# Packing the global queries of two heads into one block, w_in by halves of rows, and a new sequence of all work, in a kernel of sparse attention and a softplus layer

## The chip, the cores and the metric

The kernel runs on one core of a Trainium2 chip. TensorE (PE) multiplies, and loads its weights beside that (PEld). VectorE (DVE), ScalarE (ACT) and GpSimd (POOL) do the rest; SyncE (SP) and GpSimd issue the DMA transfers. The metric is the device time of one execution in microseconds. The time before is 339.93 us, the median of three runs (339.21, 339.93 and 340.64).

## The reference

```python
def _attn_ref(q, k, v, global_idx):           # B=8, H=8, S=576, D=64; 8 global positions
    scores = scale * np.matmul(q, k.transpose(0, 1, 3, 2))       # scale = 1/sqrt(64)
    mask = np.abs(pos[:, None] - pos[None, :]) <= 32             # a band
    mask = mask | is_global[:, None] | is_global[None, :]        # and 8 global rows and columns
    scores = np.where(mask, scores, -1000000000.0)
    scores = scores - np.max(scores, axis=-1, keepdims=True)
    attn = np.exp(scores)
    attn = attn / (np.sum(attn, axis=-1, keepdims=True) + 1e-09)
    return np.matmul(attn, v)
...
x = attn_out.transpose(0, 2, 1, 3).reshape(B * S, H * D)         # 4608 x 512
h = x @ w_in                                                     # 512 x 2048
g = np.maximum(h, 0.0) + np.log1p(np.exp(-np.abs(h)))            # softplus
return g @ w_out                                                 # 2048 x 512
```

So most queries see a band of 32 keys on either side and the 8 global keys; the 8 global queries of each head see all 576 keys.

## The kernel before

**Tiles.** A sequence of 576 tokens is cut into 18 blocks of 32. The 128 partitions hold four quarters of 32; the eight heads lie as four heads c in one half of a tile and the heads c+4 in the other. The 4608 tokens are worked through in nine phases of 512. A phase has four groups n of 128 tokens, and for each group: scores `s` (L1049) of 32 queries against their band and the global keys, mask added by VectorE (`st`, L1053), maximum `m` (L1066), subtraction (GpSimd, L1072), exponential (ScalarE, L1089), sum `sm` (L1096), reciprocal `rs` (L1098), normalization to `pn` (L1104, on GpSimd or VectorE), transpose to `pt` (VectorE, L1113). When a phase's four groups are there, PE makes the values `xo` (L1216), which are copied to `xT` (L700); then `h` (L1251, with w_in), softplus `g` (ScalarE, L1257), `o` (L1262, with w_out), a copy to `osb` and the store (L1274). The first two phases are cut into smaller pieces so that they can begin earlier, and the first four groups go another way, with the mask put into the scores by PE (L1033, L1043).

**Global queries.** Once a batch, `sg` (L941) multiplies the global queries `qg` with all keys `kx`. A quarter of rows holds the 8 queries of one head, in a block of 32 of which 8 are used; the heads of the second half (g = 1) stand in quarters rotated by one (`a ^ g`), and go to score tiles of their own. Maximum `gm` (L951), exponential `pg` (L958), transpose to `pgt` (L963), a step that writes a 1 at each global position into eight columns more (`own`, L965), then `ov` (L974), which gives the result of the global queries and, by those columns, the values at the global keys. Both become `vg`, which `xo` uses.

**Loads.** Queries, keys and values come in float32 by SP and are cast to bfloat16 (`qb`, `kb`, `vb`; L697, L695, L700, on whichever engine the order names). Batches 0 and 1 come in parts of tokens (L494, L498) and are transposed on PE (`tr`, L829; the global ones picked by `pick`, L835); the others come whole (L444, L449), are transposed by VectorE (L798, L802) and picked on PE (L858, L871). w_in (four quarters of 512 of its 2048 columns, L1313) and w_out (four quarters of rows, L1317) are issued by GpSimd. Some copies exist only to make an engine wait: on GpSimd one for a part of v of batch 0 (L1330), with the w_in issues behind it, and one for the second part of k of batch 1 (L1394), with the w_out issues behind it. On SP a tiny transfer, `trail` (L737), waits for the second quarter of w_in ahead of batch 1, and another for the first quarter of w_out ahead of batch 1's values. Matmuls `warm` (L709) fill PE's idle time at the start.

**The order.** No loop sets the order. Each piece of work is added to a list as a job, with the jobs that it needs and the buffers that it opens and uses. The tuple `ORDER` then holds numbers (5 times the job's number plus its engine), and `run` places the jobs in that sequence, each behind the last one of its engine. A model of durations in `run` decides only which PSUM bank a job gets, how many `warm` matmuls fill a gap, and in which sequence instructions are written; no engine waits for a modelled time.

## Time and profile before

| | us |
|---|---|
| runs | 339.21, 339.93, 340.64 |
| profiled execution, its span | 339.5 |
| PE busy | 319.3 (94%) |
| DVE busy | 250.8 (74%) |
| ACT busy | 222.9 (66%) |
| POOL busy | 170.9 (50%) |

A line of the page's groups reads: line of the kernel, engine, operation, output and inputs by name, partitions by elements and type, count; busy time in all, mean ns of one; idle time of the engine just before them and what ended most of it. In the timeline a row is a run of like instructions: start, length, engine, line, operation, tiles, count, and in brackets the idle time before it and what released it. "issue" there means that the profile shows nothing that the engine waited for. A busy PE is modelled, since matmuls are pipelined. Queue q0 is GpSimd's transfers, q1 is SP's, q8 the fetching of instructions.

### The profile page before, as it was taken

To read this page: it belongs to the slowest core of one execution; us is meant where nothing else is said; L and a number is where in the kernel's file an instruction comes from. 1 tells how busy PE (TensorE), PEld (TensorE's weight loads), DVE (VectorE), ACT (ScalarE), POOL (GpSimd) and SP (SyncE) were. 2 spreads that over 40 slices of the span, in tenths; PEclk is the share of its full clock that TensorE was granted. 3 is DMA by queue.
4 is the path that set the end of the run, shared out by engine and by line. 5 is a ranking of instruction groups with operands and counts; after the bars stand their busy time and mean duration, and the time that the engine had idled before them with its cause. 6 is when DMAs were issued, how large, how long until landed. Compare 5 with 4: busy or idle time off the path is not lost.

```text
span 339.5 us, 12213 instructions
## 1 busy us (share of the span) xinstructions
PE 319.3 (94%) x5336; PEld 169.4 (50%) x5336; DVE 250.8 (74%) x416; ACT 222.9 (66%) x457; POOL 170.9 (50%) x156
## 2 busy tenths in 40 slices
PE   7685967999999998999999999999999999999996
PEld 3434755466555443454455446444544554445443
DVE  7795657996798799989988979898896993441000
ACT  5695744998695757477857683768476738925442
POOL 7384705985387865715966037663514575300000
PEclk9969999999999999999999999999999999999999
DMA  7999999898946999886999995053000022001002
GB/s 183 221 179 232 207 205 171 133 192 136 152 75 105 224 182 200 143 152 130 201 174 235 168 152 133 33 119 87 4 3 31 33 93 83 16 31 66 31 15 109
DMA packets 168733, 42.74 MB, mean 126 GB/s; under 512 B 153192, under 2 KB 165736, under 8 KB 168680
## 3 DMA queue, kind: packets, MB, share of 16 engines
q1 hardware_dynamic: 160664, 28.33, 48.0%
q0 software_dynamic: 6144, 10.49, 13.0%
q10 hardware_dynamic: 1872, 3.15, 2.5%
q8 instruction: 41, 0.67, 0.8%
q14 instruction: 12, 0.10, 0.1%
HBM read 36.71 MB, written 9.44 MB: 136 GB/s over the span
## 4 chain that ended last, share of the span: by engine, by line
PE 78%; SPq 9%; DMA 7%; issue 3%; DVE 1%; ACT 1%; ACTq 0%; POOLq 0%
PE o L1262 35%; PE h L1251 32%; SPq L444 5%; PE xo L1216 4%; DMA stage<-in_v_dram 3%; PE s L1049 3%; DMA win<-in_moe_w_in_dram 2%; DMA stage<-in_k_dram 2%; PE ov L974 2%; SPq L449 1%; SPq L498 1%; DVE qb L695 1%; PE pick L858 1%; PE tr L829 1%; SPq L494 1%
## 5 line engine op out<-in xcount | busy, mean ns | idle before, releaser
L1251 PE MATMUL h<-xT,win 128*128 128x512 bf16 (+3 forms) x768 | 135.8, 326 | 4.0 <-issue 2.3
L1262 PE MATMUL o<-wout,g 128*128 128x512 bf16 (+1 forms) x592 | 136.6, 374 | 0.0
L1257 ACT ACTIVATE g<-h 128x512 bf16<-128x512 f32 (+3 forms) x192 | 85.6, 501 | 44.7 <-PE h L1251 42.7
L1251 PEld LDWEIGHTS <-win 128*128 128x128 bf16 x768 | 66.7, 98 | 63.5 <-issue 5.2
L1262 PEld LDWEIGHTS <-g 128*128 128x128 bf16 x592 | 55.7, 98 | 61.4 <-issue 1.1
L1104 POOL TENSOR_TENSOR pn<-st,rs 128x1024 bf16<-128x1024 f32 (+1 forms) x33 | 57.2, 1745 | 50.4 <-DVE rs L1098 31.8
L1072 POOL TENSOR_TENSOR st<-st,m 128x1024 f32<-128x1024 f32 x24 | 46.6, 1952 | 52.5 <-DVE m L1066 50.1
L1053 DVE TENSOR_TENSOR st<-s,mask 128x512 f32<-128x512 f32 x64 | 41.2, 678 | 12.5 <-PE s L1049 12.4
L1096 DVE TENSOR_REDUCE sm<-st 128x8 f32<-128x1024 f32 x32 | 38.2, 1195 | 7.7 <-ACT st L1089 7.7
L1066 DVE TENSOR_REDUCE m<-st 128x8 f32<-128x1024 f32 x32 | 37.9, 1199 | 0.1
L1089 ACT ACTIVATE st<-st 128x1024 f32<-128x1024 f32 x32 | 33.1, 1059 | 5.8 <-DVE st L1072 4.8
L1113 DVE STREAM_TRANSPOSE pt<-pn 128x512 int32<-128x512 int32 x36 | 24.9, 694 | 6.2 <-POOL pn L1104 6.1
L700 ACT COPY osb<-o 128x512 f32<-128x512 f32 (+1 forms) x29 | 16.7, 576 | 16.8 <-PE o L1262 15.1
L700 ACT CAST xT<-xo 128x512 bf16<-128x512 f32 (+3 forms) x27 | 11.5, 477 | 18.7 <-PE xo L1216 18.6
L700 POOL CAST vb<-stage 128x1152 bf16<-128x1152 f32 x14 | 16.9, 1215 | 9.1 <-PE xo L1216 5.4
L1049 PE MATMUL s<-kx,qx 64*32 64x128 bf16 x1152 | 15.2, 224 | 4.4 <-issue 2.6
L700 DVE CAST xT<-xo 128x512 bf16<-128x512 f32 (+3 forms) x21 | 11.3, 567 | 10.2 <-PE xo L1216 10.1
L1049 PEld LDWEIGHTS <-qx 64*32 64x32 bf16 x1152 | 10.7, 92 | 12.5 <-issue 9.9
L697 POOL TENSOR_SCALAR qb<-stage 128x1152 bf16<-128x1152 f32 (+2 forms) x12 | 12.8, 1074 | 4.7 <-DMA stage<-in_q_dram 2.4
L958 ACT ACTIVATE pg<-sg,gnb 128x320 bf16<-128x320 f32 (+1 forms) x32 | 15.0, 588 | 0.0
L1274 POOL DMA_DIRECT2D out_dram<-osb x24 | 14.7, 615 | 0.0
L951 DVE TENSOR_REDUCE gm<-sg 128x1 f32<-128x320 f32 (+1 forms) x32 | 12.3, 446 | 3.2 <-PE sg L941 3.2
(125 smaller groups left out, 311.3 us busy)
## 6 DMA issues: line engine op xcount, KB each, us to landing
stage<-in_v_dram SPq DMA_DIRECT2D x64, 144.0 KB, 4.0
stage<-in_k_dram SPq DMA_DIRECT2D x48, 144.0 KB, 4.1
stage<-in_q_dram SPq DMA_DIRECT2D x48, 144.0 KB, 3.9
out_dram<-osb POOLq DMA_DIRECT2D x24, 256.0 KB, 3.6
out_dram<-osb ACTq DMA_DIRECT2D x11, 256.0 KB, 2.0
stage<-in_k_dram SPq DMA_DIRECT2D x4, 512.0 KB, 8.2
stage<-in_q_dram SPq DMA_DIRECT2D x4, 512.0 KB, 5.5
win<-in_moe_w_in_dram POOLq DMA_DIRECT2D x4, 512.0 KB, 7.0
```

What stands on the lines that cost most here:

```text
L700: {"ACT": nc.scalar.copy, "DVE": V.tensor_copy, "POOL": nc.gpsimd.tensor_copy}[e](out, in_)
L1049: nc.tensor.matmul(out=PS["s", n, g][quad(a ^ g), x, :], lhsT=qx[b % 2][rows(g), a, j * BL:(j + 1) * BL], rhs=kx[b % 2][rows(g), a, e0 * B ...
L1053: V.tensor_tensor(out=PS["st", n][:, h, :, :], in0=PS["s", n, h][:, :, :], in1=mask[:, h, j0:j0 + PB, :, :].rearrange("p j s i -> p j (s i ...
L1066: V.reduce_max(out=m[:], in_=flat(PS["st", n], h0, h1), axis=AX)
L1072: on(e).tensor_tensor(out=t, in0=t, in1=over(PS["m", n, y][:], SL * BL), op=OP.subtract)
L1089: nc.scalar.activation(out=t, in_=t, func=AF.Exp)
L1096: V.reduce_sum(out=sm[:], in_=flat(PS["st", n], h0, h1), axis=AX)
L1104: on(e).tensor_tensor(out=PS["pn", n][:, :, :, h0:h1].rearrange("p x s h -> p h x s"), in0=PS["st", n][:, h0:h1], in1=PS["rs", n, y][:].re ...
L1113: V.transpose(out=bass.AP(base.tensor, base.offset, ap=[list(base.ap[0]), [2 * STEP, PB // 2], [STEP + BL // 2, 2], [1, SL * BL]]), in_=PS ...
L1251: nc.tensor.matmul(out=h[:, :], lhsT=w_in_t[c // 4][:, kd, c % 4 * P:(c % 4 + 1) * P], rhs=PS["xT", m][:, kd, lo:hi], start=(kd == 0), sto ...
L1257: nc.scalar.activation(out=PS["g", m, c][:, lo:hi], in_=PS[key][:, lo_of(c, hi - lo)], func=AF.Softplus)
L1262: nc.tensor.matmul(out=PS["o", m, ns, a][:, :], lhsT=PS["g", m, kf][:, ns * P:(ns + 1) * P], rhs=w_out_t[kf // 4][:, kf % 4, a:z], start=( ...
```

## The change

1. *Packing.* The heads c and c+4 stand in the same quarter c. Their global queries are the columns 0 to 7 and 8 to 15 of one block of 32, each multiplied by 1 on its own half of the partitions and by 0 on the other (a small constant, `side`, or two copies on ScalarE). One `sg` matmul of 128 rows then gives the scores of both heads: 8 matmuls a batch for 16, 2 score tiles for 4, 2 maxima for 4, 2 exponentials for 4. `pg` and `pgt` have half the columns; the weights of `ov` are read from it with a step of two.
2. *w_in.* Since a quarter c now gives heads c and c+4 to one tile of `xo`, the rows of w_in are placed to match, by eight transfers of 64 partitions where there were four of 128.
3. *The order.* ORDER is new throughout. The model that goes with it has new constants, for DMA and for fetching instructions. `warm` matmuls go from 32 to 38.

```diff
         def gev(e):
-            copy(e, qg[i][:, :, 0:NG], PS[qkey][:, QP:QP + HG * NG].rearrange("p (a g) -> p a g", g=NG))
+            x = PS[qkey][:, QP:QP + HG * NG].rearrange("p (a g) -> p a g", g=NG)
+            if e == "DVE":
+                V.tensor_tensor(out=qg[i][:, :, 0:KG].rearrange("p a (h g) -> p a h g", g=NG),
+                                in0=x.unsqueeze(2).to_broadcast([P, HG, 2, NG]),
+                                in1=side[:].unsqueeze(1).unsqueeze(3).to_broadcast([P, HG, 2, NG]), op=OP.mult)
+                return
+            for g in range(2):
+                copy(e, qg[i][rows(g), :, g * NG:(g + 1) * NG], x[rows(g)])
...
             for x, (a0, an) in enumerate(SPANS):
                 for a in range(HG):
-                    for g in range(2):
-                        rhs = kx[i][rows(g), a, (2 + 3 * a0) * BL:(2 + 3 * (a0 + an)) * BL] \
-                            .rearrange("p (c x) -> p c x", c=an)[:, :, 0:D]
-                        nc.tensor.matmul(out=PS["sg", b, g, x][quad(a ^ g), 0:an * D], lhsT=qg[i][rows(g), a, :], rhs=rhs,
-                                         start=True, stop=True)
+                    rhs = kx[i][:, a, (2 + 3 * a0) * BL:(2 + 3 * (a0 + an)) * BL].rearrange("p (c x) -> p c x", c=an)[:, :, 0:D]
+                    nc.tensor.matmul(out=PS["sg", b, x][quad(a), 0:an * D], lhsT=qg[i][:, a, :], rhs=rhs, start=True, stop=True)
...
-    pg = const([P, NJ, BL, 2], BF16, "pg")
+    pg = const([P, NO, BL, 2], BF16, "pg")
...
     def weights_in(x):
-        nc.gpsimd.dma_start(out=w_in_t[x][:, :, :],
-                            in_=moe_w_in.rearrange("(a p) f -> p a f", p=P)[:, :, x * WC:(x + 1) * WC])
+        for g in range(2):
+            nc.gpsimd.dma_start(out=w_in_t[x][rows(g), :, :],
+                                in_=moe_w_in.rearrange("(g a d) f -> g d a f", g=2, d=D)[g, :, :, x * WC:(x + 1) * WC])
...
-        42, 47, 116, 92, 9, 121, 126, 111, 132, 52, 107, 137, 102, 97, 143, 83, 148, 158, 87, 152, 178, 14, 221, 19,
...
```

What the new order does is read from the instructions of the two programs. GpSimd, from the w_in issues to the first subtraction, before (the tile win_124 is w_in's first quarter, wout_128 w_out's; stage_61 holds k, stage_60 q, stage_62 v):

```order
25 L1313 DMA win_125<-in_moe_w_in_dram 128x4x512
26 L700 CAST vb_66<-stage_62 128x18x64 x2
27 L1313 DMA win_126<-in_moe_w_in_dram 128x4x512
28 L1104 TENSOR_TENSOR pn<-st,rs 128x512 x3
29 L1313 DMA win_127<-in_moe_w_in_dram 128x4x512
30 L1104 TENSOR_TENSOR pn<-st,rs 128x512 x3
31 L513 MEMSET kx_71 128x40x16
...
35 L1394 COPY seen<-stage_61 128x1
36 L700 CAST kb<-stage_61 128x2x4x64
37 L1317 DMA wout_128<-in_moe_w_out_dram 128x4x512
```

and of the change:

```order
26 L1245 DMA win_130<-in_moe_w_in_dram 64x4x512 x2
27 L1245 DMA win_131<-in_moe_w_in_dram 64x4x512 x2
28 L652 CAST vb_66<-stage_62 128x18x64
29 L1245 DMA win_132<-in_moe_w_in_dram 64x4x512 x2
30 L1039 TENSOR_TENSOR pn<-st,rs 128x512 x3
31 L1325 COPY seen<-stage_61 128x1
32 L1249 DMA wout_133<-in_moe_w_out_dram 128x4x512
33 L1249 DMA wout_134<-in_moe_w_out_dram 128x4x512
34 L462 MEMSET kx_71 128x40x16
...
39 L1249 DMA wout_135<-in_moe_w_out_dram 128x4x512
40 L652 CAST kb<-stage_61 128x2x4x64 x2
```

All w_in issues now stand ahead of the normalizations of phase 0, the blanking of `kx` behind the copy that waits, and the casts of the second half of batch 1's keys behind three w_out issues instead of ahead of all. The last w_out issue stands behind four casts of q before (row 43), and behind two and the first subtraction now (also row 43).

PE, where batch 1's keys are transposed, before:

```order
882 L1251 MATMUL h<-xT,win_124 128x128
883 L829 LDWEIGHTS kb
884 L829 MATMUL tr<-ident,kb 128x128
...
914 L835 MATMUL pick<-hot,kb 128x8
915 L1251 LDWEIGHTS win_126
```

and of the change:

```order
1044 L1149 MATMUL xo<-pt,vb_66 64x32
1045 L1183 LDWEIGHTS win_131
...
1100 L1183 MATMUL h<-xT,win_132 128x128
1101 L774 LDWEIGHTS kb
1102 L774 MATMUL tr<-ident,kb 128x128
```

The first transposes of batch 1 stood ahead of the second 88 values of phase 0 (rows 929 to 1104), and those of the keys' second half directly behind; now those values (rows 869 to 1044) and 28 h matmuls stand ahead of the transposes, and the second half of the keys follows at row 1150.

SP, at the start, before (k, its small parts, q, its small parts, q, then v):

```order
2 L494 DMA stage_61<-in_k_dram 128x8x128 x2
3 L498 DMA stage_61<-in_k_dram 64x4x64 x2
4 L494 DMA stage_60<-in_q_dram 128x8x128
5 L498 DMA stage_60<-in_q_dram 64x4x64 x2
6 L494 DMA stage_60<-in_q_dram 128x8x128
7 L449 DMA stage_62<-in_v_dram 32x18x64 x8
```

and of the change:

```order
2 L443 DMA stage_60<-in_q_dram 128x8x128
3 L447 DMA stage_60<-in_q_dram 64x4x64 x2
4 L443 DMA stage_61<-in_k_dram 128x8x128
5 L447 DMA stage_61<-in_k_dram 64x4x64 x2
6 L443 DMA stage_61<-in_k_dram 128x8x128
7 L398 DMA stage_62<-in_v_dram 32x18x64 x4
```

q now leads, and half of v comes ahead of the second part of q.

More of the change, by code (lines that the diff above doesn't have):

```diff
@@ L100, in room @@
[L100 to L111 removed]
+            t0 = max(t0, free[want - 1])
+        return t0
@@ new lines, in stall @@
+    def stall(self, t, took, ins):
+        held, n = 0, self.issued
+        asked, need, due, last = self.fetch
+        due = list(due)
+        while n + ins >= min(asked, need):
+            at = min(asked, need)
+            here = t + held + took * max(at - n, 0) / max(ins, 1)
+            if at == asked:
+                ask = max(here, last - self.USABLE)
+                last = ask + self.FETCH + max([0] + [
+                    self.HEAVY if x["queue"] and x["each"] <= 100 else next(wait for each, wait in self.WAIT if x["each"] > each)
+                    for x in self.dma if x["to"] > ask + 200 and x["from"] < ask + 1500])
+                due.append(last)
+                asked += self.BLOCK
+            else:
+                held += max(0, due.pop(0) - here)
+                need += self.BLOCK
+        return held, (asked, need, due, last)
@@ L112, in settle, with advance @@
+    def advance(self, s, until):
+        lines = self.lines
+        while any(s["at"][q] < len(lines[q]) for q in range(2)) and s["now"] < until:
+            due = [1e12, 1e12]
+            for q in range(2):
+                if s["at"][q] < len(lines[q]):
+                    due[q] = max(lines[q][s["at"][q]]["ask"] + self.START[q], s["ok"][q])
+            on = [t <= s["now"] + 1e-9 for t in due]
             if not any(on):
-                now = min(due)
+                if min(due) >= until:
+                    return
+                s["now"] = max(s["now"], min(due))
@@ L121, in settle @@
+            if not any(on):
+                continue
+            rate = [1.0 * x for x in on]
+            if all(on):
+                each = [lines[q][s["at"][q]]["each"] for q in range(2)]
+                rate = [x / sum(each) for x in each]
+            step = until - s["now"]
             for q in range(2):
                 if on[q]:
-                    left[q] -= step * rate[q]
-            now += step
+                    step = min(step, s["left"][q] / rate[q])
+                elif due[q] < 1e11:
+                    step = min(step, max(due[q] - s["now"], 1e-6))
@@ L136, in keep, with transfer @@
+    def transfer(self, j, t):
+        q = int("POOL" in j["cost"])
+        n, each = j["moves"]
+        self.advance(self.base, t - 4000)
+        x = dict(queue=q, ask=t, work=n * each, each=each, job=j if j["lands"] else None, to=1e18)
+        x["from"] = 0
+        self.dma.append(x)
+        self.lines[q].append(x)
+        self.advance({k: list(v) if isinstance(v, list) else v for k, v in self.base.items()}, 1e11)
     def keep(self, t0, t1, order):
@@ L155, in keep @@
         order.append(j)
-    def size(self, j):
-        return j["ins"] or 2
-    def follow(self, places):
-        engines = ("PE", "ACT", "DVE", "POOL", "DMA")
-        self.given = [(x // 5, engines[x % 5]) for x in places]
     def due(self, j):
@@ new lines, in due, with run @@
+        return max(t, self.room(j["opens"])) if j["opens"] else t
+    def run(self, places, free):
+        engines = ("PE", "ACT", "DVE", "POOL", "DMA")
+        order, table, array = [], "exp", 128
+        self.dma, self.lines = [], ([], [])
+        self.base = dict(at=[0, 0], left=[-1, -1], ok=[-1, -1], now=0)
+        self.fetch, self.issued = (self.ASK, self.NEED, [], 0), 0
+        mine, other = (0, 0), (0, 0)
+        for place in places:
+            j, e = self.jobs[place // 5], engines[place % 5]
+            t = max(self.due(j), free[e])
+            step, took = j["cost"][e]
@@ L324 @@
     KG = 2 * NG
+    NO = NJ // 2
     VW = 2 * D + 2
@@ L1402 @@
         make_batch(batches(us)[-1] + 1)
-    o.follow(ORDER)
-    for job in o.run(dict(PE=1200 if WARM else 3000, ACT=2600, DVE=2100, POOL=3400, DMA=2300)):
+    for job in o.run(ORDER, dict(PE=1200, ACT=2600, DVE=2100, POOL=3400, DMA=2300)):
         job["emit"](job["on"])
```

456 lines of the change are left out of this document (175 added, 281 removed), and 133 rows, old and new, of the table ORDER.

## The prediction

> **What bounds the kernel now.** I read the page first: the span, the busy shares and the 40 slices.
>
> ```profile
> span 339.5 us, 12213 instructions
> PE 319.3 (94%) x5336; PEld 169.4 (50%) x5336; DVE 250.8 (74%) x416; ACT 222.9 (66%) x457; POOL 170.9 (50%) x156
> PE   7685967999999998999999999999999999999996
> ```
>
> TensorE is busy for 94% of the span, and the digits below 8 stand only in the first seven slices, which are 8.5 us each. From there on it is the bound. So a change of order can win only what stands idle at the front, and the small gaps behind it. The stretches tell how much that is (us, then busy time and number of instructions of PE, PEld, DVE, ACT, POOL; then PEclk, DMA share, GB/s):
>
> ```profile
> 26.30:44.60 18.30, 14.03 (x348) 11.60 (x340) 11.13 (x28) 12.13 (x48) 9.73 (x18) 1.00 1.15 218
> 44.60:55.02 10.42, 5.62 (x141) 3.93 (x140) 6.02 (x8) 4.23 (x12) 2.92 (x2) 1.00 1.22 197
> 55.02:140.00 84.98, 82.86 (x1648) 46.41 (x1649) 74.78 (x114) 64.38 (x127) 57.70 (x40) 1.00 0.87 155
> 90.00:250.00 160.00, 158.04 (x2860) 79.13 (x2858) 145.42 (x215) 109.31 (x175) 95.43 (x69) 1.00 0.71 136
> ```
>
> Between 26.3 and 55.0 us PE stands idle for 4.3 + 4.8 = 9.1 us, from 55 to 140 us for 2.1 us in all. The last row is a warning: there VectorE is busy for 145.4 of 160 us, the second engine close to its bound.
>
> What the 9.1 us are, by PE's timeline (start, us, engine, line, operation, count, then the idle time before it and what ended it):
>
> ```profile
> 28.52 2.67 PE L1251 MATMUL h<-xT,win 128*128 128x128 bf16 x44 [1.62 <-ACT xT L700]
> 33.41 0.40 PE L829 MATMUL tr<-ident,kb 128*128 128x128 bf16 x4 [2.22 <-DVE kb L700]
> 47.45 0.66 PE L1049 MATMUL s<-kx,qx 64*32 64x128 bf16 x53 [2.63 <-issue]
> 55.02 0.34 PE L1251 MATMUL h<-xT,win 128*128 128x128 bf16 x3 [2.17 <-issue]
> ```
>
> One wait of 2.22 us is for keys of batch 1, which stand ahead of the values of phase 0. Two waits, 2.63 and 2.17 us, end on "issue": PE waited for no other engine. How many instructions PE had issued by then says what they are (stretches from 0):
>
> ```profile
> 0.00:40.80 40.80, 30.71 (x607) 18.64 (x607) 30.66 (x88) 29.40 (x112) 26.97 (x57) 0.92 1.09 207
> 0.00:44.82 44.82, 34.56 (x735) 21.79 (x735) 32.58 (x93) 32.09 (x122) 27.57 (x57) 0.92 1.10 204
> 0.00:52.85 52.85, 39.96 (x863) 25.66 (x863) 37.55 (x101) 35.74 (x132) 28.84 (x58) 0.94 1.12 204
> ```
>
> 607, 735 and 863 of each kind: the steps are 128 + 128 = 256 instructions, exactly. The page's queue of instructions moves 41 packets for 10672 instructions of PE, again about 260 to a packet. So PE runs dry at a block of code that is fetched by DMA. In the windows 44.7 to 47.4 us and 52 to 55 us the queues show why it is late:
>
> ```profile
> q8 instruction: 41, 0.67, 0.8%
> q0 software_dynamic: 547, 0.54, 121.9%
> q8 instruction: 1, 0.02, 2.2%
> q1 hardware_dynamic: 2046, 0.51, 111.7%
> q8 instruction: 1, 0.02, 2.9%
> ```
>
> The first row is the page's, over the span. In each window one packet of code goes through engines that w_out (q0), then v (q1) keep wholly busy. The Trainium skill ("Runtime: NRT & Kernel Launch", section "Instruction fetch mechanics") gives the block as 256 instructions, and the trace agrees; it calls the crossing "mostly hidden", and here two crossings cost 4.8 us.
>
> **The change part by part.** *Packing the global queries.* Four reductions and four exponentials a batch become two and two; the transpose halves from 576 to 288 columns, the maximum behind it too.
>
> ```profile
> L951 DVE TENSOR_REDUCE gm<-sg 128x1 f32<-128x320 f32 (+1 forms) x32 | 12.3, 446 | 3.2 <-PE sg L941 3.2
> L958 ACT ACTIVATE pg<-sg,gnb 128x320 bf16<-128x320 f32 (+1 forms) x32 | 15.0, 588 | 0.0
> L963 DVE STREAM_TRANSPOSE pgt<-pg x9: 446/726/779, 21.3 to 268.1; 128x576 int32<-128x576 int32 x7, 128x320 int32<-128x320 int32 x1, 128x256 int32<-128x256 int32 x1
> L965 DVE TENSOR_REDUCE pgt<-own x9: 285/452/453, 21.8 to 268.9; 128x288 bf16<-128x288 bf16 x7, 128x160 bf16<-128x160 bf16 x1, 128x128 bf16<-128x128 bf16 x1
> L941 PE MATMUL sg<-kx,qg x128: 267/306/436, 15.9 to 262.6; 64*32 64x320 bf16 x64, 64*32 64x256 bf16 x64
> ```
>
> VectorE saves 2 x 0.446 = 0.89 us a batch. The transpose of 288 columns lies next to the one of 256, which is the 446 ns; I take 0.47 for 0.726, so 0.25 us. The maximum goes the same way from 0.452 to about 0.30, 0.15 us. That is 1.3 us a batch, 10 us in all. ScalarE saves 2 x 0.588 = 1.2 us a batch if an activation stays as long (its output is written with a step as before); were it twice as long, nothing. On PE, 16 matmuls on quarter tiles, eight at a time, become 8, four at a time: two rounds either way, so nothing, with bounds from half a round to a round of 0.31 us a batch: -1.2 to +2.5 us. Directly the part is worth zero, since PE does not wait for VectorE there. The order hands the time out again: VectorE gets six more normalizations from GpSimd, so its load stays about equal, and GpSimd's falls by some 10 us.
>
> *w_in by halves of rows.* Eight transfers of 256 KB for four of 512 KB:
>
> ```profile
> L1313 POOL DMA_DIRECT2D win<-in_moe_w_in_dram x4: 751/786/992, 16.2 to 25.0; - x4
> DMA to landing us min/median/max: 5.9/7.0/8.2
> ```
>
> GpSimd pays 4 x 0.786 = 3.1 us more of issuing. The issues now run from about 16.2 to 23, with a cast between, where the last of before was at 25.0, because three normalizations no longer stand ahead of it; the last quarter, 5.9 to 8.2 us later by the row, lands at 29 to 31 us for 31 to 33 before. The first h matmuls, which used two other quarters first and now go through all four, then start at 28.5 to 29.4, at most 0.9 us late; what follows waits for other things (below), so I count 0, with bounds 0 to +0.9. The Trainium skill ("DMA: Bandwidth & Descriptors", section "Rules for kernel authors") speaks against it: two transfers to disjoint halves of the partitions serialize, and one over 128 should be used. By that rule both halves together land when the one did, and the sum keeps only the issuing; no run here shows a split one yet.
>
> *The front.* The values of phase 0 (88 matmuls) now stand ahead of the transposes of batch 1 instead of behind the first of them. Behind 36 h matmuls of 0.061 us (2.67/44) from 29.4 they start at about 32 us, where PE of before stood waiting. So the 2.22 us are filled with work. What comes late next is the second half of batch 1's keys, cast on GpSimd:
>
> ```profile
> 28.76 0.80 POOL L513 MEMSET kx<- 128x640 int32 x3
> 35.01 0.44 POOL L1394 COPY seen<-stage 128x1 f32<-128x1 f32 x1 [5.30 <-DMA stage<-in_k_dram]
> 35.40 0.61 POOL L700 CAST kb<-stage 128x512 bf16<-128x512 f32 x1
> 35.95 2.29 POOL L1317 DMA_DIRECT2D wout<-in_moe_w_out_dram  x3
> 51.58 1.89 POOL L1072 TENSOR_TENSOR st<-st,m 128x1024 f32<-128x1024 f32 x1 [10.18 <-DVE m L1066]
> ```
>
> In the new order GpSimd does: the copy that waits (35.01 + 0.44), two w_out issues (1.53), the memsets that were done at 28.76 before (0.80, and some 0.2 for two small ones), a small cast (about 0.4), a third issue (0.76), the cast (0.61). The sum is 39.8 us. PE asks for it at row 1150 of its order, which it reaches at about 37, so a new wait of up to 3 us stands there. The fetch goes on meanwhile, so that the block at row 1470, for which PE of before waited 2.63 us, is there when PE comes, at 39.8 and 7.6 us of work (rows 1150 to 1470 by the durations of before): about 47.4, the clock of before. But by then the new order has put 2.2 us more work through: 72 and 56 h matmuls of 128 and 256 columns for 64 and 36 (20 x 0.109, half of the 0.217 that 512 columns take, below). At the next block, row 1726, it is 1.3 us ahead (more h, fewer s). That block came 7.5 us behind its forerunner before; with the forerunner at 45 to 47, it is there at 52 to 54.5 for 55.02. So the front wins from 1.3 + 0.5 to 1.3 + 3.1 us, 1.8 to 4.4. I take 2.4, near the low end, since w_out still fills the engines at the same time. Bounds: -1 (w_out's last quarter, issued behind the first subtraction of phase 1, comes late by as much as was won and 1 us more) to +5 (both waits on code gone).
>
> *Behind the front.* Of the 2.1 us idle between 55 and 140 us, GpSimd's lighter load and earlier casts can fill about half: -1.1, bounds 0 to -2.1. The matmuls on small tiles are in fewer groups, 85 for 92 changes of the tile's form after the front. One change is worth what these rows leave:
>
> ```profile
> 56.87 0.38 PE L1262 MATMUL o<-wout,g 128*128 128x512 bf16 x1
> 59.53 2.11 PE L1262 MATMUL o<-wout,g 128*128 128x512 bf16 x9
> 61.57 0.44 PE L941 MATMUL sg<-kx,qg 64*32 64x320 bf16 x16
> 61.94 2.33 PE L1262 MATMUL o<-wout,g 128*128 128x512 bf16 x10
> ```
>
> One o takes 0.38, ten take 2.33, so each next one (2.33 - 0.38)/9 = 0.217. Nine are through at 59.53 + 1.95 = 61.48, and sg starts at 61.57: 0.09 us. Seven fewer give -0.7 (0.1 each, rounded up).
>
> Against this stands batch 3. Its queries and keys are picked some 10 us of PE's work earlier than before (row 3385 of its order for 3953). The views show, of before, that pick, the load and the cast ahead of it, and the page's row of such loads with KB and us to landing:
>
> ```profile
> 112.48 0.46 PE L858 MATMUL pick<-kb,pick 128*32 128x128 bf16 x17
> 87.52 8.62 SPq L444 DMA_DIRECT2D stage<-in_q_dram  x8
> 108.89 1.47 POOL L697 TENSOR_SCALAR qb<-stage 128x1152 bf16<-128x1152 f32 x1
> stage<-in_q_dram SPq DMA_DIRECT2D x48, 144.0 KB, 3.9
> ```
>
> PE will ask at 112.5 - 10.2 - 2.4 = 99.9 us. The last of eight loads is issued by 96.1 and lands 3.9 us later, and a cast takes 1.5: 101.5, if SP issues no earlier. What the front wins may bring SP forward too, so the wait is 0 to 1.6 us: +0.5.
>
> Sum: -2.4 - 1.1 - 0.7 + 0.5 = -3.7 us, a span of 335.8. The profiled execution has a span of 339.5, the runs a median of 339.93, so 0.4 us lie around it: 336.2 us.
>
> **The rivals.** *The front gives nothing.* The block of code at row 1726 is late again by what the order has put ahead, because w_out is still moving when it is asked for. For it speaks that both windows show the engines full and that no byte less is moved; against it that the two asks now fall at other times. Then only -1.1 - 0.7 + 0.5 remain, and if VectorE, at 145 of 160 us, delays the values as soon as PE runs ahead, not even those: 338.6 to 339.9. The skill's sentence that fetching is mostly hidden, taken for the cause of nothing, leads to the same time.
>
> *Both blocks are in time.* If the new times of w_out's issues leave the asks free, the 4.8 us go, and with -1.3 for the rest: 333.8, or 332 with all gaps behind filled.
>
> *Slower: the casts of batch 3.* Should q of batch 3 be cast where it was cast before, until 110.4 us, PE, asking at 99.9, waits for 10.5 us: 346.7. The point from which it decides is 103.6 us, where a wait of 3.7 us takes back all. For it speaks that ScalarE's and VectorE's queues at that place are as full as before; against it that their rows were moved along with PE's. The same holds, at a smaller price, for w_out's last quarter. Its transfers landed so long after their issue (L1317):
>
> ```profile
> DMA to landing us min/median/max: 7.7/10.4/11.9
> ```
>
> It is issued behind GpSimd's first subtraction, which was over at 53.5, so it lands at 61.2 to 65.4 us, for a use at about 62: 0 to 3.4 us.
>
> **How the numbers follow.** The forecast (334.8 to 338.2) has 0.52, both blocks in time (331.5 to 334.8) 0.14, no gain at the front (338.2 to 341.6) 0.21, slower (beyond) 0.13. The measurement tells no less than 0.5%, 1.7 us, from no change. So faster 0.66, same 0.21, slower 0.13. The range runs from 332.0, both blocks in time and half the gaps filled, to 340.5, which leaves out most of the slower case and little else.
>
> **What would show it.** Right: PE's timeline has 88 xo at about 32 us, a wait of up to 3 us for kb that ends near 39.8, waits on "issue" whose sum between 40 and 60 us is under 3 us, and gm and pg groups of 16 instructions with means near 446 and 588 ns. Wrong: "issue" waits of 4.8 us or more in the front, a wait for qb at the picks near 100 us of over 2 us, a wait for wout near 62 us, or pg activations that take twice as long.

## The result: slower by 3.9%

The changed kernel takes 353.62 us (median of 4 runs, 351.70 to 354.25) where the kernel before, run beside it, takes 340.28: a ratio of 1.039, with a 95% interval from 1.0345 to 1.0436. The forecast was 336.2 us, the range ended at 340.5. The profiled execution took 353.99 us, 352.3 of them its span. In all that follows, a ratio goes by the faster runs of each kernel (those within 1.5% of its fastest), and the traces of the new code in the old order, of the first run of w_in by halves and of the four held pieces alone are of longer runs, so that only their rows are used, not their spans, and whether the faster runs had the same waits is not shown. From the page, the busy times and PE's 40 slices:

```profile
PE 320.4 (91%) x5236; PEld 173.2 (49%) x5278; DVE 257.7 (73%) x416; ACT 219.4 (62%) x444; POOL 156.9 (45%) x153
PE   7667979989997998999799999999779999999996
```

PE's work is the same (320.4 us busy, 319.3 before). The holes are new, and they lie where there were none: digits of 7 stand in the middle and near the end of the second row, where before every slice behind the seventh read 9, but for one 8 and the last, a 6 (the prediction left the last one out). VectorE's busy time did not stay equal; it rose from 250.8 to 257.7 us, while GpSimd's fell by 14.

Behind the front, PE's timeline has six waits of about 1 us and more, where before it had one (0.96 us, at 131):

```profile
78.06 0.38 PE L1149 MATMUL xo<-pt,vg 32*64 32x384 bf16 x8 [1.07 <-DVE pt L1048]
113.83 0.38 PE L1194 MATMUL o<-wout,g 128*128 128x512 bf16 x1 [1.98 <-issue]
140.72 0.80 PE L916 MATMUL ov<-vb,pgt 32*32 32x129 bf16 x72 [1.68 <-DVE pgt L907]
141.68 4.44 PE L1194 MATMUL o<-wout,g 128*128 128x512 bf16 x12 [0.16 <-issue]
174.12 0.80 PE L916 MATMUL ov<-vb,pgt 32*32 32x129 bf16 x72 [1.98 <-DVE pgt L907]
253.23 0.38 PE L1149 MATMUL xo<-pt,vg 32*64 32x384 bf16 x8 [1.34 <-DVE pt L1048]
257.23 0.27 PE L1149 MATMUL xo<-pt,vb 32*64 32x96 bf16 x17 [2.48 <-issue]
```

The six sum to 10.5 us. The row at 141.68 is another kind of loss, not a wait: twelve o matmuls in 4.44 us, where ten took 2.33 us before. The granted clock says why. Stretches of the changed kernel, the columns as in the prediction (PEclk is the third from the end):

```profile
245.00:265.00 20.00, 15.63 (x310) 8.06 (x312) 16.25 (x22) 8.37 (x17) 9.60 (x8) 0.91 0.15 54
258.00:261.00 3.00, 2.67 (x69) 1.55 (x70) 3.00 (x5) 1.98 (x3) 0.85 (x1) 0.50 0.02 5
```

and of the kernel before:

```profile
245.00:265.00 20.00, 20.00 (x277) 9.58 (x263) 16.62 (x24) 13.97 (x22) 6.52 (x5) 1.00 0.05 16
```

From 258 to 261 us PE runs at half its clock. There are three such stretches of 3.4 us behind the front (from 114.5, 141.8 and 257.8 us), each 0.6 to 1.1 us behind the end of a wait, and each costs half its length, 1.7 us: 5.1 in all. So 10.5 + 5.1, less the 2.1 us of gaps that only the kernel before has there, is 13.5, where the span grew by 12.8; the 0.7 us between them I leave open. The two executions, laid beside each other where they have equal work left (matmuls weighted by their columns, an estimate), give the same picture: level at 57 us, then 1.3 us lost by 78, 4.6 by 118, about 5 by 149, 7.6 behind the wait at 174, and 12.8 from 264 to the end.

**Two causes stand behind the six waits.** Four end on VectorE. Pieces ahead of them there and on GpSimd, and two rows by name (minimum, median and maximum ns):

```profile
68.10 7.46 POOL L1039 TENSOR_TENSOR pn<-st,rs 128x1024 bf16<-128x1024 f32 x4
71.00 1.18 DVE L1031 TENSOR_REDUCE sm<-st 128x8 f32<-128x1024 f32 x1
73.84 2.38 DVE L652 CAST kb<-stage 128x1152 bf16<-128x1152 f32 x1
126.80 2.08 POOL L652 CAST kb<-stage 128x1152 bf16<-128x1152 f32 x1
127.44 2.05 DVE L652 CAST vb<-stage 128x1152 bf16<-128x1152 f32 x1
128.80 1.70 POOL L652 CAST vb<-stage 128x1152 bf16<-128x1152 f32 x1
165.47 5.60 POOL L1007 TENSOR_TENSOR st<-st,m 128x1024 f32<-128x1024 f32 x3
168.67 3.58 DVE L1039 TENSOR_TENSOR pn<-st,rs 128x1024 bf16<-128x1024 f32 x1
249.37 1.90 POOL L1039 TENSOR_TENSOR pn<-st,rs 128x1024 bf16<-128x1024 f32 x1 [0.82 <-DVE pt L1048]
249.59 2.84 DVE L1039 TENSOR_TENSOR pn<-st,rs 128x1024 bf16<-128x1024 f32 x1
L1039 DVE TENSOR_TENSOR pn<-st,rs x13: 698/1301/3578, 28.3 to 312.7; 128x1024 bf16<-128x1024 f32 x8, 128x512 bf16<-128x512 f32 x5
L652 DVE CAST vb<-stage x4: 749/754/2053, 21.9 to 273.4; 128x1152 bf16<-128x1152 f32 x4
```

A normalization that takes VectorE 1.3 us by the median takes 3.58 and 2.84 here, a cast of 0.75 takes 2.38 and 2.05. Each of the slow ones started while GpSimd was at work, and ended about its own time behind the end of a piece of GpSimd's: 168.67 + 3.58 = 172.25 is 1.18 us behind GpSimd's end at 171.07; 249.59 + 2.84 = 252.43 is 1.16 behind 251.27; the cast at 73.84 ends 0.66 behind 75.56, the one at 127.44 ends 0.61 behind 128.88. The reduction at 71.00, under the same chain as the cast at 73.84, kept its 1.18 us. So VectorE's normalizations and casts are held until a piece of GpSimd's is through, and its reductions are not. From each of the held pieces to the end of the wait behind it VectorE had hardly any idle time (0.14 us at most), and what they took over their kind, 1.6, 2.2 (two casts, of 1.71 and 2.05 us), 2.3 and 1.5 us, is more than the waits, 1.07, 1.68, 1.98 and 1.34. Over VectorE's normalizations, subtractions and casts, the time above the median of the same operation and shape sums to 11.8 us in the changed kernel and 4.7 in the one before; without it, by this estimate, VectorE's load is the same in both, 246 us, as forecast. The Trainium skill ("SBUF — State Buffer", section "Who interferes with whom") says that VectorE with two inputs in SBUF contends with a GpSimd instruction that reads SBUF, that the later one fully blocks, and that reductions never contend. The trace agrees. In one point it is not of one kind: the page lets the lock go with each instruction, and the cast at 127.44 did get in behind one cast of GpSimd's, whose next one then took 1.70 us; but the normalization at 168.67 waited through the end of the second subtraction (169.2) and the whole third.

The other two waits, at 113.83 and 257.23, are the blocks of 256 instructions again. How many weight loads PE had issued at a wait on "issue" (stretches from 0; weight loads are counted, since 42 matmuls are missing from this trace):

```profile
0.00:51.90 51.90, 38.41 (x731) 25.66 (x733) 34.55 (x98) 32.97 (x124) 23.31 (x59) 0.90 1.12 198
0.00:113.80 113.80, 95.71 (x1999) 61.34 (x2013) 90.12 (x182) 75.48 (x218) 67.32 (x88) 0.96 1.02 178
0.00:257.20 257.20, 229.66 (x4283) 128.46 (x4314) 212.36 (x352) 167.91 (x362) 146.90 (x147) 0.97 0.82 152
```

From 733 to 2013 is 10 x 128 exactly, and from there to 4314 is 18 x 128 less 3. What such waits have in common is a burst of short instructions ahead: the 143 values from 253.23 on and their loads were through in 1.5 us, and then PE stood for 2.48 us until the block was there. Here the DMA engines were full during the burst (0.93 from 252.5 to 254.5 us) and empty behind it; an experiment below has such waits with the engines nearly empty throughout.

### The profile page after: what moved, and what is told of

It is laid out like the page before. It is cut to its first block, busy times and chain, and to the rows that moved or that the text cites. A ratio compares the mean times of both kernels' runs of the same rounds, so it can differ in the third digit from the quotient of the medians.

```text
span 352.3 us, 12026 instructions
## 1 busy us (share of the span) xinstructions
PE 320.4 (91%) x5236; PEld 173.2 (49%) x5278; DVE 257.7 (73%) x416; ACT 219.4 (62%) x444; POOL 156.9 (45%) x153
## 4 chain that ended last, share of the span: by engine, by line
PE 74%; DVE 10%; ACT 5%; issue 5%; SPq 3%; DMA 2%; POOL 1%; DVEq 0%; ACTq 0%
PE h L1183 31%; PE o L1194 31%; PE xo L1149 4%; PE s L984 3%; ACT st L1020 2%; DMA stage<-in_q_dram 2%; DVE pn L1039 2%; PE ov L916 1%; SPq L398 1%; DVE kb L652 1%; DVE sm L1031 1%; DVE m L1001 1%; SPq L447 1%; PE pick L803 1%; DVE pt L1048 1%
## 5 line engine op out<-in xcount | busy, mean ns | idle before, releaser
L1183 PE MATMUL h<-xT,win 128*128 128x512 bf16 (+3 forms) x760 | 138.1, 332 | 2.9 <-issue 2.5
L1194 PE MATMUL o<-wout,g 128*128 128x512 bf16 (+1 forms) x560 | 132.2, 377 | 5.7 <-issue 5.0
L1189 ACT ACTIVATE g<-h 128x512 bf16<-128x512 f32 (+3 forms) x192 | 83.2, 505 | 44.0 <-PE h L1183 42.1
L1183 PEld LDWEIGHTS <-win 128*128 128x128 bf16 x768 | 68.9, 100 | 65.5 <-issue 7.7
L1039 POOL TENSOR_TENSOR pn<-st,rs 128x1024 bf16<-128x1024 f32 (+1 forms) x27 | 48.4, 1803 | 82.4 <-DVE rs L1033 57.6
L1007 POOL TENSOR_TENSOR st<-st,m 128x1024 f32<-128x1024 f32 x23 | 43.5, 1898 | 38.0 <-DVE m L1001 37.8
L1024 ACT ACTIVATE st<-st 128x1024 f32<-128x1024 f32 x32 | 32.6, 1051 | 2.7 <-POOL st L1007 2.5
L1039 DVE TENSOR_TENSOR pn<-st,rs 128x1024 bf16<-128x1024 f32 (+1 forms) x13 | 18.4, 1427 | 0.2
L652 POOL CAST kb<-stage 128x1152 bf16<-128x1152 f32 (+2 forms) x11 | 14.7, 1349 | 8.5 <-DMA stage<-in_k_dram 8.5
L1149 PE MATMUL xo<-pt,vb 32*64 32x96 bf16 (+2 forms) x1328 | 14.3, 210 | 3.3 <-issue 3.3
L649 POOL TENSOR_SCALAR qb<-stage 128x1152 bf16<-128x1152 f32 (+1 forms) x8 | 10.2, 1290 | 15.0 <-DMA stage<-in_q_dram 14.7
L984 PEld LDWEIGHTS <-qx 64*32 64x32 bf16 x1152 | 10.8, 94 | 10.5 <-issue 7.1
```

The costliest lines, as they stand in the source:

```text
L652: {"ACT": nc.scalar.copy, "DVE": V.tensor_copy, "POOL": nc.gpsimd.tensor_copy}[e](out, in_)
L984: nc.tensor.matmul(out=PS["s", n, g][quad(a), x, :], lhsT=qx[b % 2][rows(g), a, j * BL:(j + 1) * BL], rhs=kx[b % 2][rows(g), a, e0 * BL:(e ...
L1007: on(e).tensor_tensor(out=t, in0=t, in1=over(PS["m", n, y][:], SL * BL), op=OP.subtract)
L1024: nc.scalar.activation(out=t, in_=t, func=AF.Exp)
L1039: on(e).tensor_tensor(out=PS["pn", n][:, :, :, h0:h1].rearrange("p x s h -> p h x s"), in0=PS["st", n][:, h0:h1], in1=PS["rs", n, y][:].re ...
L1183: nc.tensor.matmul(out=h[:, :], lhsT=w_in_t[c // 4][:, kd, c % 4 * P:(c % 4 + 1) * P], rhs=PS["xT", m][:, kd, lo:hi], start=(kd == 0), sto ...
```

## The experiments

All kernels below compute the whole result; where narrow matmuls are added, they are extra work on a few columns that nothing reads.

**The new code in the old order.** The changed functions, with the order of before:

```diff
-ORDER = [the changed kernel's]
+ORDER = [the kernel before's]
```

> The changed kernel with the old sequence: packing and w_in by halves are in, the sequence is the old one. Theory A (the loss of 13 us lies in the new sequence, in five places where VectorE or a block of code came late, and in the half-clock stretches behind them): 338 to 343 us, near the 340.3 of before, with the front's two waits on code of 2.6 and 2.2 us still there, possibly at other rows, since 16 instructions a batch are gone. Theory B (packing or the split of w_in costs the time by itself, by weights read with a step of two or exponentials written with a step): 348 us or more, and the global queries' steps longer than 0.45 us for a maximum and 0.59 us for an exponential.

Measured 352.43 us (349.15 to 356.96), ratio 1.026 [1.0204, 1.0318]. Without any of the new order, two thirds of the loss was there. But the groups of the packed queries were not the cause, and PE's waits were of the other kind:

```profile
L910 ACT ACTIVATE pg<-sg,gnb 128x320 bf16<-128x320 f32 (+1 forms) x16 | 8.1, 583 | 0.0
PE xo L1159 <- issue: 6.9, 5, 2.8
188.47 0.55 PE L1159 MATMUL xo<-pt,vb 32*64 32x96 bf16 x35 [2.75 <-issue]
```

The activations are as short as before (588 ns) and half as many. The four longest waits on "issue" stand at instructions 5304, 6328, 7352 and 8632 of PE (twice its weight loads so far), which are all 184 past a multiple of 256, each in the middle of a run of values. Packing takes 16 instructions a batch out of PE's program, and so moves every later border. Theory A had that for the front alone; it led to the next two runs.

**The same, with the borders put back.** Eight narrow matmuls a batch take the place of the eight removed, and the counts of the warming matmuls are set so that each piece of work has the row number on PE that it had before:

```diff
+            for y in range(8):
+                nc.tensor.matmul(out=PS["sg", b, 0][quad(y % HG), 0:8], lhsT=qg[i][:, y % HG, :],
+                                 rhs=kx[i][:, y % HG, 2 * BL:2 * BL + 8], start=True, stop=True)
```

> The changed kernel with the old sequence, as in the first experiment, but with 8 narrow matmuls (8 columns, writing again what the scores of the global queries hold) a batch in place of the 8 that packing removed, and with as many filling matmuls as the old kernel: every instruction of PE has the number that it had in the old kernel. Theory A (packing with the old sequence lost its 11 us because 16 instructions fewer a batch moved the block boundaries into the bursts of values): the waits on issue at the values, 6.9 us in sum, fall below 0.5 us, the half-clock stretches behind them go, time 340 to 346 us, the rest over 340.9 being the late keys of batch 1 (4.3 us of waiting for 2.2). Theory B (packing costs by itself): 349 us or more.

Measured 344.60 us (343.29 to 346.39), ratio 1.0146 [1.008, 1.0211]. The kernel issues more instructions and is faster, by the two ratios 1.15% or 3.9 us. Between 57 and 300 us one wait over 0.8 us is left, and it is VectorE's. In the profiled execution, the shortest of the four, what remains over the kernel before, 1.7 us of span, is at the front, where PE waits longer for keys (5.23 us for 2.22; why they come later was not traced), and the wait at 78.91 is made good again by 149 us:

```profile
36.35 0.61 PE L787 MATMUL tr<-ident,kb 128*128 128x128 bf16 x4 [5.23 <-DVE kb L662]
78.91 0.38 PE L1164 MATMUL xo<-pt,vg 32*64 32x384 bf16 x8 [1.51 <-DVE pt L1063]
```

**The borders alone, on the kernel before.** Forty narrow matmuls, with their loads 80 instructions, once, in batch 2:

```diff
+            for y in range(40 if b == 2 else 0):
+                nc.tensor.matmul(out=PS["sg", b, 0, 0][quad(y % HG), 0:8], lhsT=qg[i][rows(0), y % HG, :],
+                                 rhs=kx[i][rows(0), y % HG, 2 * BL:2 * BL + 8], start=True, stop=True)
```

> The kernel before, with 40 narrow matmuls (80 instructions, some 0.5 to 1 us) in the global queries of batch 2 and nothing else. Theory A (the old kernel had its block boundaries where no burst of short matmuls met them, and any other place costs): waits on issue of 1.5 to 4 us appear at the values of four phases, near 147, 182, 217 and 253 us, 8 to 12 us in sum, with half-clock stretches of 3.4 us behind some of them: 349 to 358 us. Theory B (the boundaries matter only at the front, where w_out and v fill the DMA engines): 340 to 342 us.

Measured 360.88 us (360.36 to 365.64), ratio 1.064 [1.0557, 1.0719]: some 20 us for 40 narrow matmuls, and more than the expectations had.

```profile
PE s L1052 <- issue: 12.3, 5, 3.3
151.03 0.41 PE L1052 MATMUL s<-kx,qx 64*32 64x128 bf16 x16 [2.52 <-issue]
188.46 0.35 PE L1052 MATMUL s<-kx,qx 64*32 64x128 bf16 x13 [3.32 <-issue]
224.91 0.28 PE L1052 MATMUL s<-kx,qx 64*32 64x128 bf16 x9 [2.30 <-issue]
262.87 0.24 PE L1052 MATMUL s<-kx,qx 64*32 64x128 bf16 x6 [2.11 <-issue]
220.50:224.90 4.40, 2.11 (x185) 1.68 (x183) 2.87 (x4) 3.30 (x4) 1.14 (x1) 1.00 0.03 9
258.50:262.80 4.30, 2.26 (x218) 1.89 (x219) 3.73 (x6) 1.07 (x2) 2.24 (x2) 1.00 0.02 6
188.40:193.00 4.60, 4.54 (x26) 1.79 (x26) 4.08 (x5) 0.26 (x1) 1.15 (x1) 0.63 0.46 109
```

The shift puts borders into the runs of s matmuls of the later batches. The four new waits sum to 10.2 us. Ahead of the last two and during them, the DMA engines were busy for 0.03 and 0.02 of the time (the two stretches above), so full engines are not needed for such a wait. The clock falls behind the waits: the last row, a stretch, has a mean of 0.63, and the whole span 0.967 for 0.990 (the first 57 us 0.94 in both), which is (0.033 x 359.2) - (0.010 x 339.5) = 8.5 us of full speed. That names 18.7 of the 19.7 us that the span grew. Two waits for ScalarE and VectorE at 115 and 117 us, just behind the added matmuls, make 1.8 more than the one of 0.50 that stood there before; that its front was 1.5 us ahead of the other's takes about as much off.

**The changed kernel, its last border moved.** Sixteen narrow matmuls ahead of the program's first gap, 32 instructions:

```diff
+            for x in range(16):
+                nc.tensor.matmul(out=ps[:, 0:8], lhsT=idle[:, 0, :], rhs=idle[:, 0, 0:8], start=True, stop=True)
```

> The changed kernel with 16 more matmuls of 8 columns in the first gap of PE, so that every block boundary lies 32 instructions earlier in the program; nothing else. Theory A (the waits on issue at 113.8 and 257.2 us are blocks of 256 instructions asked for just ahead of a burst of some 270 short matmuls): the wait of 2.48 us at the last values of batch 6 falls below 0.8 us, because its block is asked for some 7 matmuls before PE stands waiting there; the one of 1.98 us at 113.8 stays between 1 and 3, since its block is asked for while the loads fill the DMA engines; new waits under 1 us may come elsewhere. Time 349.5 to 352.5 us for 353.6. Theory B (these waits have to do with the work around them, not with where 256 instructions end): both waits stay within 0.3 us, time 353 to 355.

Measured 351.71 us (350.99 to 353.34), ratio 1.033 [1.027, 1.0389]. The wait of 2.48 us near 257 is gone, the four waits for VectorE are as they were, and the border near 113 fell worse, not better:

```profile
112.55 0.25 PE L1155 MATMUL xo<-pt,vb 32*64 32x32 bf16 x7 [3.57 <-issue]
```

I had expected 1 to 3 us there. So a shift trades borders; by the two ratios this one gained some 2 us, and the intervals overlap.

**The held pieces taken off VectorE.** Five numbers of the order change their engine and nothing else: casts of k of batches 2 and 4 and of v of batch 3 to ScalarE, two normalizations to GpSimd. They are the held pieces ahead of the four waits (the two casts that belong to the wait at 140.72 stand 11 us ahead of it).

```diff
-        ... 2782, ... 4492, ... 3882, ... 4622, ... 6287, ...
+        ... 2781, ... 4491, ... 3881, ... 4623, ... 6288, ...
```

> The changed kernel with five pieces of work taken off VectorE, at the same place of the sequence: three casts (k of batches 2 and 4, v of batch 3) to ScalarE, two normalizations (groups 18 and 25) to GpSimd. These five took 2.38, 1.71, 2.05, 3.58 and 2.84 us on VectorE where others of their kind took 0.8 or 1.2, each while GpSimd worked on tensors of its own. Theory A (VectorE and GpSimd hold each other up, and PE's waits of 1.07, 1.68, 1.98 and 1.34 us at 78, 140.7, 174 and 253 us stand behind these five): the four waits fall from 6.1 us to under 1.5 us in sum, the clock falls to half less often, time 344 to 348.5 us. Theory B (VectorE simply has too much to do, 258 us busy, and the sequence pushes it through PE's needs): the waits move to other places and fall by less than 2 us in sum, time 351 to 354.

Measured 342.21 us (340.31 to 344.86), ratio 1.0044 [1.0003, 1.0085]: five pieces of some 400 on VectorE bring back 11.4 us, more than expected. Behind 57 us, these are all the waits of 0.8 us or more that are left:

```profile
110.78 0.39 PE L1204 MATMUL o<-wout,g 128*128 128x512 bf16 x1 [1.50 <-issue]
125.53 2.75 PE L1193 MATMUL h<-xT,win 128*128 128x512 bf16 x12 [1.35 <-ACT g L1199]
247.11 0.27 PE L1159 MATMUL xo<-pt,vb 32*64 32x96 bf16 x17 [1.46 <-issue]
```

The four waits were 6.1 us. The two waits on borders also became shorter (4.46 to 2.96), and the mean clock rose from 0.971 to 0.985 (the first 57 us 0.91 in both), which is (0.029 x 352.3) - (0.015 x 340.8) = 5.1 us. With a new wait of 1.35 that makes 11.4, where the spans differ by 11.5. But laid beside the kernel before as above, this execution was some 2 us ahead at 57 us already, and 9.5 of the 11.5 lie behind it; so the list is some 2 us too long, which I leave open. That the borders cost less when PE isn't stopped just before is seen, not explained.

**The control: four other pieces.** As many pieces as in the next kernel, of the same kinds, but ones that GpSimd did not hold: a subtraction and a normalization to GpSimd, a cast of q of batch 6 and of v of batch 5 to ScalarE.

```diff
-        ... 4697, ... 4712, ... 5592, ... 6212, ...
+        ... 4698, ... 4713, ... 5591, ... 6211, ...
```

> The changed kernel with four other pieces taken off VectorE: a subtraction and a normalization (both of group 20) to GpSimd, a cast of q of batch 6 and one of v of batch 5 to ScalarE. These are of the same kinds as the four of the eighth kernel, but each took what its kind takes (1.2, 1.3, 0.8 and 0.8 us), so none was held up by GpSimd. Theory A (VectorE's holding up by GpSimd at four places is what PE waits behind): the four waits of 1.07, 1.68, 1.98 and 1.34 us stay within 0.5 us each, time 351 to 355 us. Theory B (VectorE has too much to do, and any 4 us less would do): 347 us or less.

Measured 352.73 us (351.74 to 353.81), ratio 1.035 [1.03, 1.0406]: nothing gained. The long normalizations and the waits behind them are there as before:

```profile
L1049 DVE TENSOR_TENSOR pn<-st,rs x12: 703/1286/3599, 25.9 to 311.1; 128x1024 bf16<-128x1024 f32 x7, 128x512 bf16<-128x512 f32 x5
169.95 0.80 PE L926 MATMUL ov<-vb,pgt 32*32 32x129 bf16 x72 [2.00 <-DVE pgt L917]
251.27 0.38 PE L1159 MATMUL xo<-pt,vg 32*64 32x384 bf16 x8 [1.33 <-DVE pt L1058]
```

So 4 us less work on VectorE at these other places is worth nothing. The control is weaker than it looks in one respect: its four pieces stood at 174 to 203 us, behind three of the four waits, so that they could not have shortened those. Taking pieces that were not held from just ahead of the waits was not tried. That it is the holding and not just any work at those places rests on the sizes above: at each wait the time over the piece's kind is more than the wait.

**Four held pieces, and the borders moved on top.** Without the cast of v, in three forms: alone; with 25 narrow matmuls in batch 3 and nine warming ones fewer; with 108 narrow matmuls in one gap of the front and 36 in batch 3.

```diff
+            for y in range(25 if b == 3 else 0):
+                nc.tensor.matmul(out=PS["sg", b, 0][quad(y % HG), 0:8], lhsT=qg[i][:, y % HG, :],
+                                 rhs=kx[i][:, y % HG, 2 * BL:2 * BL + 8], start=True, stop=True)
```

> The changed kernel with the four pieces taken off VectorE and no matmul added or left out: the sixth kernel without its shifts of the block boundaries. Theory A (the two shifts are worth the waits on issue at 109 and 245 us, 1.9 and 1.5 us, less 1.3 us that they put at 78.8; the wait of 1.4 us for ScalarE goes by leaving the cast of v where it was): both waits are back, the time is 340.5 to 342.5 us. Theory B (the shifts did nothing, the gain of the sixth kernel over the third came from the cast alone): 339.5 to 340.5 us.

> The changed kernel with four pieces taken off VectorE (the third experiment's without the cast of v of batch 3, which stays), nine filling matmuls fewer at the front (block boundaries 18 instructions later from there on) and 25 narrow matmuls in the global queries of batch 3 (boundaries 32 instructions earlier from there on). Theory A: of the third experiment's waits, 1.5 us at the values of batch 6 go, 1.9 us at 109 us fall below 1.2, the wait of 1.4 us for ScalarE at 124 us goes: time 337 to 341 us for its 342.2. Theory B (what is left after the third experiment does not hang on block boundaries): 341.5 to 343 us.

> The four pieces taken off VectorE, 108 narrow matmuls of 8 columns in a gap of 3 us that PE has at 7 us (boundaries 216 instructions earlier, which is 40 later to the next), and 36 in the global queries of batch 3 (then 288, or 32 earlier). Theory A (the boundaries alone decide the waits on issue behind 57 us): the waits at 78.8, 109 and 245 us stay under 0.5 us each, time 336.5 to 340 us. Theory B (another wait takes their place, since every shift puts boundaries near other bursts): a wait on issue of 1.5 us or more elsewhere behind 57 us, time 340 to 344 us.

Measured 342.35 us (ratio 1.0008 [0.9967, 1.0049]), 340.50 (1.0006 [0.9971, 1.0042]) and 341.66 (0.9992 [0.9951, 1.0032]). The four pieces alone bring the changed kernel level with the one before. Moving the borders takes the waits of 2.01 and 1.67 us near 112 and 248 away and makes one nearer the front, in the second form and in the third:

```profile
78.80 0.27 PE L1198 MATMUL h<-xT,win 128*128 128x128 bf16 x2 [1.29 <-issue]
79.90 0.35 PE L818 MATMUL pick<-kb,pick 128*32 128x128 bf16 x9 [1.34 <-issue]
```

In time the three can't be told apart, so the theory that better borders would give a further gain here isn't borne out; each kernel's own runs lie 4 to 6 us apart.

**w_in by halves, on the kernel before.** The change's transfer alone, run twice:

```diff
-        nc.gpsimd.dma_start(out=w_in_t[x][:, :, :],
-                            in_=moe_w_in.rearrange("(a p) f -> p a f", p=P)[:, :, x * WC:(x + 1) * WC])
+        for g in range(2):
+            nc.gpsimd.dma_start(out=w_in_t[x][rows(g), :, :],
+                                in_=moe_w_in.rearrange("(a p) f -> p a f", p=P)[rows(g), :, x * WC:(x + 1) * WC])
```

> The kernel before with w_in fetched by eight transfers of 64 partitions where it had four of 128; nothing else. Theory A (the split costs only GpSimd's issuing, four more of 0.65 to 0.8 us): the last quarter is issued 3 us later, at about 28, and lands at 34 to 36 us, the first h matmuls wait a little, time 340 to 343 us. Theory B (the split is a cause of the loss, by slower transfers in halves): over 345 us, landings of the halves beyond 9 us.

> The fourth kernel again, with more rounds: the kernel before with w_in fetched by halves. Theory A (the split is neutral within what a measurement tells): ratio 0.996 to 1.003. Theory B (the split helps a little): ratio below 0.996 with the upper end of its interval below 1.

Measured 339.33 us (336.95 to 344.52), ratio 0.9961 [0.9922, 0.9999], and 340.48 (335.85 to 345.08), ratio 0.9923 [0.988, 0.9967].

```profile
L1314 POOL DMA_DIRECT2D win<-in_moe_w_in_dram x8: 619/636/852, 16.1 to 25.9; - x8
DMA to landing us min/median/max: 4.0/6.8/8.1
```

The rows are of the first run. Each issue is shorter than that of a whole quarter (786 ns), and by the median the halves land no later than the whole did (7.0 us); the last landing took 8.1 us in the first run and 9.4 in the second, for 8.2. The split costs nothing that shows. The second ratio is what the expectation called a small help, but whether it gains is not settled: the medians of all runs differ by 1.6 and 0.6 us, less than either kernel's spread.

## Why the prediction was wrong

**The step that failed is "Behind the front".** Its terms were -1.1 for gaps that GpSimd's lighter load would fill and -0.7 for fewer changes of the tiles' form (no run shows that one by itself). That stretch lost 12.8 us. The page's warning, VectorE 145.4 of 160 us, was read as a bound on how far PE could gain, never as a price. What the sum left out:

- *"The order hands the time out again", counted as free.* Normalizations on VectorE went from 7 to 13, casts of v from 0 to 4. By their median durations that is what packing saved, and so the load was put as "about equal". But a piece's duration on VectorE depends on what GpSimd does beside it. Rows of the kernel before show that (below the list). What the held pieces cost is shown by the two kernels that moved them: 9 to 11 us, with the borders and the clock that followed them.
- *Packing on PE, "worth zero".* As work it was. As 16 instructions a batch fewer it moved every later border between blocks of code, and in the old order that cost some 4 us, the difference that putting them back made (the two were run on different chips, and their intervals overlap a little; the waits on "issue" that vanish among the values carry it).
- *"One packet of code goes through engines that w_out, then v keep wholly busy", as the cause of the waits on code.* Too narrow. Full engines may lengthen the way of a block, but by these runs a burst of short instructions ahead of a border is enough; in the kernel before with 40 narrow matmuls two such waits came with the engines at 0.03 and 0.02. With the narrow cause, I looked for borders only where weights move.
- *The clock.* No term allowed for it, since it stood at 1.00 behind the front. Behind new waits it did not.

The rows of the kernel before, with the one wait behind its front:

```profile
L1104 DVE TENSOR_TENSOR pn<-st,rs x7: 724/1305/2086, 28.6 to 300.0; 128x1024 bf16<-128x1024 f32 x5, 128x512 bf16<-128x512 f32 x2
126.58 3.75 POOL L1072 TENSOR_TENSOR st<-st,m 128x1024 f32<-128x1024 f32 x2
128.10 2.90 DVE L695 TENSOR_SCALAR qb<-stage 128x1152 bf16<-128x1152 f32 x1 [0.22 <-DMA stage<-in_v_dram]
131.05 0.47 PE L858 MATMUL pick<-qb,pick 128*32 128x128 bf16 x18 [0.96 <-DVE qb L695]
```

A maximum of 2.1 us for a normalization of 1.3, and a cast of 2.90 us where its kind takes 0.8, asked for their cause. The cast ended 0.67 us behind GpSimd's two subtractions, and PE waited for it.

**The front: -2.4 predicted, and no gain shown.** The changed kernel was level with the one before at 57 us. Six variants with its front, compared in the same way, were ahead there by 0.7 to 2.7 us. But executions with the front of before differ as much among themselves: the one with 40 narrow matmuls in batch 2, whose front is the same, was ahead by 1.5, and the second of w_in by halves by 2.3. Why the front varies that much from one execution to the next stays open, and a gain of 2.4 us can't be told from it. The steps to that sum were wrong for the most part:

```profile
10.65 0.40 PE L774 MATMUL tr<-ident,kb 128*128 128x128 bf16 x4 [2.62 <-ACT kb L652]
32.78 3.71 PE L1183 MATMUL h<-xT,win 128*128 128x128 bf16 x36 [0.21 <-ACT xT L652]
41.48 0.39 PE L774 MATMUL tr<-ident,kb 128*128 128x128 bf16 x4
```

q is loaded first, so the first keys were transposed at 10.65 us, for 6.56 before; that order of SP's loads stands in the part on the change, and I priced none of it. The first h matmuls came at 32.8 us, not at 28.5 to 29.4, and 36 of them took 3.71 us, 0.103 each for the 0.061 that I had used, since the granted clock stood at 0.50 from 32.6 to 36.0 us. The wait of up to 3 us for batch 1's keys near 39.8 did not come: PE got there at 41.5 and found them. The waits on code at the front, 4.8 us before, became 0.85, 0.45 and 1.29, so that "under 3 us" held. Late by the loads and early by the borders: where a variant came near the forecast's -2.4, that was luck.

**What was right.** The packed groups themselves:

```profile
L900 ACT ACTIVATE pg<-sg,gnb 128x320 bf16<-128x320 f32 (+1 forms) x16 | 8.0, 569 | 1.2 <-DVE gnb L895 0.8 <-DVE rs L1033 0.4
L894 DVE TENSOR_REDUCE gm<-sg 128x1 f32<-128x320 f32 (+1 forms) x16 | 6.5, 443 | 0.3 <-PE sg L888 0.3
```

Sixteen each, 569 and 443 ns for the 588 and 446 forecast, the transpose at 0.47 and the maximum at 0.30 us where it stands at 173. w_in's halves at nothing in the sum (their issuing cost GpSimd 1.9 us more, not 3.1, since an issue of a half took 0.64 us). VectorE's load was right too, if the time in which it was held is left out. The slower rival's mechanism, the casts of batch 3, didn't occur: its picks started at 103.8 us without a wait, and +0.5 for them wasn't needed. The kernel got slower by another way, one that no rival described. The rival that came nearest named VectorE, but priced it at no gain instead of a loss.

## What to carry to other kernels

Before work is moved to an engine, look at the spread of that operation's durations there, not at its mean: a maximum far above the median can be a second engine holding it, and then the new place decides how often that happens. Where an engine runs through its program in long bursts of short instructions, treat the position of each block of 256 instructions as part of the schedule: a change that adds or removes instructions early has to be read at all later borders. And a stretch without idle time gives a new order little to gain and much to lose; price it by what each newly placed piece may wait for.

## What the runs showed of the hardware

- VectorE's normalizations and casts that start while GpSimd works are held: they ended 1.16 and 1.18 us (normalizations) and 0.61 and 0.66 us (casts) behind the end of a piece of GpSimd's. Its reductions are not (1.18 us under the same chain). Whether VectorE gets in behind the first piece differs: a cast did at 128.9, a normalization waited for the end of a second subtraction (3.58 us for 1.3). What decides it was not tested.
- A block of instructions for PE can come late with the DMA engines nearly empty (0.03 and 0.02). Such waits cost up to 3.6 us here, and 80 instructions more in one place made the kernel before 20 us slower. The Trainium skill ("Runtime: NRT & Kernel Launch", section "Instruction fetch mechanics") calls a crossing mostly hidden. Most of the crossings in these traces show no wait either; the long waits stood where a border fell into a burst of short matmuls or just behind one.
- A wait of 1.7 to 2.5 us can cost another 1.7, since PE then runs at half its clock for 3.4 us. It isn't certain to: behind the wait of 1.98 us at 174 in the changed kernel the clock stayed at 1.00, and in the control, behind the like wait at 170, the mean of the 15 us from there was 0.89. The Trainium skill ("TensorE: Matmul & The Clock Gate", section "Part 1: The HAM clock gate (the "warmup" mystery)") gives the window as about 3.4 us, free-running, and half the clock after at least one idle window. The length of the stretches agrees, and so does free-running: the three starts lie 27.3 and 116.0 us apart, 8 and 34 times 3.41. The condition doesn't, for the waits were shorter than a window.
